# The lead of an attention-and-MLP kernel: a copy and two read-outs change engine, three loads change places, and an order is planned anew

## The chip, the cores and the metric

The kernel runs on one core of a Trainium2 chip. The core has a matrix engine (PE), a vector engine (DVE), an activation engine (ACT) and a general one (POOL); SP issues the DMAs. Each engine works through its own list of instructions in order, and waits on semaphores for the others. The metric is the device time of one execution in microseconds (us); less is better.

## The reference, cut to what matters

Two batches of 8 heads, 768 positions, 64 values per head. Each query attends to a window of 31 neighbours and, besides, to 24 block summaries (the maximum of the keys, the mean of the values, over blocks of 32). The result goes through two MLPs.

```python
k_sum = k.reshape(B, H, nb, 32, D).max(axis=3)
v_sum = v.reshape(B, H, nb, 32, D).mean(axis=3)
scores_l = scale * q @ k.T                    # masked to |i - j| < 16
scores_s = scale * q @ k_sum.T + log(32)
a = softmax(concat(scores_l, scores_s))
x = a @ concat(v, v_sum)                      # 1536 tokens x 512
x = (relu(x @ w_in) ** 2) @ w_out             # MLP 1
out = silu(x @ w_in2) @ w_out2                # MLP 2
```

## The kernel before, in words

The 12 attention tiles of a batch hold 64 queries each; their keys are 96 neighbours and the 24 summaries, 120 in all. The first eight tiles are the **lead**: nothing else can run before them, since MLP 1 works on their 512 tokens (`gemm1 0` is its first product, tile `h`). The other tiles are done in pairs between the products of MLP 1. After the lead PE has work without a gap.

One tile of the lead passes through these steps. The names are those of the planner; in brackets the names that the profile shows.

- `psl (g, hp)` on PE: scores of tile g for a pair of heads (`pss<-kws,qrlead`), two matmuls. `kwl (hp, i)` on ACT lays the window keys of tiles 0 to 3 or 4 to 7 side by side (`kws<-t_ksum`); `ksum` and `ksl` on DVE put the summaries of the keys beside them.
- `ttl (g, hp)` on DVE: mask and minimum, read from PSUM (`T<-pss,cst_sb`; the mask is in `cst_sb`). `exl (g, hp)` on ACT: exponential and its sum (`T<-T,m`). `ze`, `rc`, `nt` on DVE: guard, reciprocal and four scalings (`z`, `r`, `T<-T,r`).
- `psa g` on PE: four transposes (`psa<-cst_sb,T`). `a g`: the copy of them out of PSUM (`a<-psa`, 120x512), on ACT.
- `vs c`, c from 0 to 5, on PE: the sums of the values (`psv<-vrows,share`), for all tiles together. `vmean 0` and `vmean 1` on ACT copy them four times each into rows 96 to 119 of `vlead`, for tiles 0 to 3 and 4 to 7 (`vlead<-psv`, 24x2048); in the code that is a source whose outer step is zero.
- `av g` on PE: eight products (`av<-a,vlead`). `xh g` on ACT and `xl g` on DVE: the high and the low part of the result (`xt<-av`). `gemm1 0` reads all eight pairs.

Beside this, weights are prepared in steps `sc` (ACT), `sh` and `st2` (DVE), `hi` (ACT, `wi` or `wo`) and `lo` (DVE); `vfm` on ACT (`vfr<-vlead`, 24x512) puts the sums of the values in place for later tiles; `vend` on PE, and `vfc` on DVE behind it (`vfr<-vsum`), do the like for the second batch, whose first tiles begin with `av 12`.

The order of all this is set by `first_order`. It lists every step with its engine, a duration, a due time and what it needs, and then plays the program through: whenever an engine is free it takes, among the steps that could start soonest, the one with the earliest due time. The instructions are then written out in that order. A due time or a duration that changes thus moves other steps too. Loads are all issued by SP, in the order of a list. Before the first scores PE runs ten matmuls of zeros (`idle_out`), and between the groups of scores six and four more.

Of the kernel before, what the change touches and what calls it, by code (L numbers as in the profile page):

```python
# [10 lines left out]
F32 = mybir.dt.float32  # L11
F32R = mybir.dt.float32r
AF = mybir.ActivationFunctionType
# [9 lines left out]
P = 128  # L23
# [22 lines left out]
NLEAD = 8  # L46
# [7 lines left out]
NRING = 8  # L54
NMIXED = 2
FIRST2 = 1
DEC1 = 14
# [9 lines left out]
def first_order():  # L67
# [6 lines left out]
    def op(eng, name, arg, dur, due, deps=(), bank=None, kb=0):  # L74
        o = index[name, arg] = dict(eng=eng, name=name, arg=arg, dur=dur, due=due + shift.get(name, 0), deps=list(deps), bank=bank, kb=kb,
                                    n=len(ops))
        ops.append(o)
# [7 lines left out]
    def pair(name, g):  # L85
        return g if g < NLEAD + 2 * (name == "pss") else g // 2 * 2
# [12 lines left out]

    for i, (name, arg, kb) in enumerate([("kt", 0, 393), ("q", 0, 524), ("kt", 1, 393), ("cst", 0, 250), ("kt", 2, 393),  # L100
                                         ("kt", 3, 393), ("q", 1, 524), ("vr", 0, 524), ("vr", 1, 524), ("vr", 2, 524),
                                         ("vl", 0, 1150), ("vl", 1, 1150)]):
        load(name, arg, kb, -100 + i)
    for hp in range(NHP):
        op("vec", "ksum", hp, 1.0, -50 + hp, [("kt", hp, 0)])
        for i in range(NLEAD // NGRP):
            op("act", "kwl", (hp, i), .5, -50 + hp + 51 * i, [("kt", hp, 0)])
            op("vec", "ksl", (hp, i), .13, -50 + hp + 48 * i, [("ksum", hp, 0)])
    for c in range(6):
        op("pe", "vs", c, .92, 2.7 + .1 * c, [("vr", c // 2, 0)])  # L110
    for i in range(NLEAD // NGRP):
        op("act", "vmean", i, 1.9, -5, [("vs", c, M) for c in range(6)] + [("vl", i, 0)] * 0)
    for i in range(NVF):
# [9 lines left out]
    for g in range(NFIRST):  # L123
# [24 lines left out]
        visit("psa", g, .62, due - 2, [("nt", g, -.1)], ("att", "a", g))  # L148
        op("act", "a", g, .56, due, [("psa", pair("psa", g), M)] + [("av", pair("av", g - 2), M)] * (g >= NLEAD + 2))
        values = [("vl", g // NGRP, 0), ("vmean", g // NGRP, A)] if g < NLEAD else [("vf", g, 0), ("vfm", g % NVF, A)]  # L150
# [6 lines left out]
    for i, (x, s) in enumerate(chunks):  # L157
# [4 lines left out]
        if i >= NSPL:  # L162
            y = chunks[i - NSPL]
            before += [("lo", y, A)] + [("scr", y[1], 0)] * (y[0] == "wo")
        op("act", "sc", (x, s), .59, due, [("raw", (x, s), 0)] + before)
        op("vec", "sh", (x, s), .35, due, [("raw", (x, s), 0)])
        op("vec", "st2", (x, s), .61, due, [("sh", (x, s), 0), ("sc", (x, s), A)])
# [14 lines left out]

    free = dict(sp=0.0, act=0.0, vec=0.0, pool=2.0, pe=5.6)
    end, banks, moved = {}, dict(att=[], acc=[]), 2.0
# [37 lines left out]
def kernel(  # L222
# [239 lines left out]
    def a_copy(g):  # L462
        d = st[g]
        a = d.pop("pa")[0:NK].rearrange("p c q -> p (c q)")
        if g >= NLEAD:
            d["a"] = p2.tile([P, 512], F32, tag="a", bufs=2, name=f"a{g}")
        copy(act, d["a"][0:NK], a)

# [133 lines left out]
    def first_block():  # L602
# [6 lines left out]
        psv = ps_h.tile([P, DM], F32, tag="h", name="psv0")  # L609
        vec.memset(idle_in.bitcast(F32), 0.0)  # L610
        def turn(n):
            for _ in range(n):
                mm(idle_out, idle_in[:, 0:P], idle_in, start=True, stop=True)
# [64 lines left out]
        def vmean(i):  # L678
            means = psv[NWIN:NK]
            copy(act, vlead[NWIN:NK, i * NGRP:i * NGRP + NGRP].rearrange("p g h d -> p g (h d)"),  # L680
                 bass.AP(means.tensor, means.offset, [means.ap[0], [0, NGRP], means.ap[1]]))
# [474 lines left out]
```

## Time and profile before

| | |
|---|---|
| time, median of 3 runs | 587.97 us (587.80 to 588.05) |
| the profiled execution, its own time | 587.53 us |
| its span, first to last instruction | 585.7 us |
| PE busy | 577.5 us, 99% |
| DVE, ACT, POOL busy | 384.8, 363.1, 95.3 us |
| the chain that ended last, by engine | PE 95%, ACT 2%, DVE 1%, DMA 1% |
| granted TensorE clock, mean | 1.000 |

How to read it: the span is 1.8 us shorter than the time of the same execution; what lies around it is start and end. The chain is followed back from the last instruction, at each step to what released it. The share of an engine over the whole span says little on the lead, which is the first 6% of it; the stretches of 10 us and the rows in order of time, shown below, do.

### The profile page before, as it was taken

Reading aid. Unit: us, or ns where it says so; the run is one execution under the profiler, and the core shown is the slowest. Engines: PE = TensorE matmul, PEld = TensorE weight load, DVE = VectorE, ACT = ScalarE, POOL = GpSimd, SP = SyncE. Lnnn points to the kernel's source line nnn. Section 1 sums busy time; section 2 is a strip of 40 time slices with the busy share of each in tenths; the row PEclk is TensorE's granted clock in tenths of the full one; section 3 lists DMA queues with packets and bytes.
Section 4 is the critical chain, followed back from the end, with each engine's and each line's share of the span. In section 5 each row is a group of like instructions: output and inputs, shape, how many; then the busy total and the mean of one; then the engine's idle time right before and its main releaser. Section 6 shows DMA issues by size and latency. Waiting matters only on the chain.

```text
span 585.7 us, 9518 instructions
## 1 busy us (share of the span) xinstructions
PE 577.5 (99%) x3300; PEld 489.4 (84%) x3300; DVE 384.8 (66%) x975; ACT 363.1 (62%) x848; POOL 95.3 (16%) x99
## 2 busy tenths in 40 slices
PE   8989999999999999999999999999999999999997
PEld 7578888878888888888888889999889888889995
DVE  6989899852867556286553688676665765666641
ACT  6999797954736554385455677665555655555541
POOL 0001101103553443076342300000000000000000
PEclk9999999999999999999999999999999999999999
DMA  9999989753988879526870112242248311111002
GB/s 316 303 305 307 346 289 325 250 166 127 319 304 293 288 258 340 178 92 196 287 261 28 36 55 73 90 145 90 91 144 358 145 36 37 36 37 35 23 17 107
DMA packets 42240, 104.42 MB, mean 178 GB/s; under 512 B 4560, under 2 KB 11856, under 8 KB 42192
## 3 DMA queue, kind: packets, MB, share of 16 engines
q1 hardware_dynamic: 42192, 103.81, 52.2%
q8 instruction: 26, 0.43, 0.3%
q14 instruction: 22, 0.18, 0.1%
HBM read 78.37 MB, written 25.43 MB: 177 GB/s over the span
## 4 chain that ended last, share of the span: by engine, by line
PE 95%; ACT 2%; DVE 1%; DMA 1%; issue 0%; DVEq 0%; ACTq 0%
PE acc L256 45%; PE h L256 23%; PE hx L256 11%; PE hz L256 6%; PE pss L256 4%; PE hy L256 3%; PE psa L460 2%; PE av L256 1%; ACT T L423 1%; ACT vlead L260 1%; DMA t_ksum<-in_kT_dram 1%; DVE xt L264 0%; PE idle_out L256 0%; PE psv L256 0%; ACT L260 0%; ACT a L260 0%
## 5 line engine op out<-in xcount | busy, mean ns | idle before, releaser
L256 PE MATMUL h<-xt,wi 128*128 128x512 f32 x576 | 143.0, 394 | 1.2 <-ACT xt L260 0.9
L256 PE MATMUL acc<-g,wo 128*128 128x512 f32 x576 | 140.4, 391 | 0.0
L256 PE MATMUL acc<-wq,g 128*128 128x512 f32 x576 | 134.3, 390 | 0.0
L256 PEld LDWEIGHTS h<-xt,wi 128*128 128x128 f32 x576 | 106.7, 188 | 24.7 <-ACT xt L260 1.0
L256 PEld LDWEIGHTS acc<-g,wo 128*128 128x128 f32 x576 | 107.4, 188 | 22.5 <-issue 0.2
L256 PEld LDWEIGHTS acc<-wq,g 128*128 128x128 f32 x576 | 107.8, 188 | 21.9 <-DVE wq L264 0.3
L264 DVE TENSOR_TENSOR g<-r,g 128x512 fp32r<-128x512 f32 x48 | 38.5, 802 | 68.4 <-ACT g L260 37.5
L264 DVE TENSOR_TENSOR r_s<-v,r_s 128x256 fp32r<-128x256 f32 x48 | 20.6, 432 | 66.6 <-ACT r_s L260 66.6
L260 ACT ACTIVATE e<-hx 128x384 f32<-128x384 f32 x32 | 15.7, 492 | 61.9 <-PE hx L256 61.8
L423 ACT ACTIVATE T<-T,m 128x120 f32<-128x120 f32 x96 | 36.6, 383 | 8.4 <-DVE m L418 8.3
L260 ACT ACTIVATE g<-s 128x384 fp32r<-128x384 f32 x64 | 32.9, 517 | 10.3 <-DVE s L264 10.2
L256 PE MATMUL hx<-x_t,r_s 128*128 128x384 f32 x192 | 38.5, 335 | 0.0
L264 DVE TENSOR_TENSOR g<-s,g 128x384 fp32r<-128x384 f32 x64 | 35.1, 553 | 2.6 <-ACT g L260 1.1
L256 PEld LDWEIGHTS hx<-x_t,r_s 128*128 128x128 f32 x192 | 33.8, 188 | 0.3
L968 ACT ACTIVATE s<-e 128x384 f32<-128x384 f32 x48 | 25.0, 522 | 8.7 <-DVE e L264 6.4
L264 POOL TENSOR_TENSOR wo<-c_wo,wo 128x512 fp32r<-128x512 f32 x16 | 25.9, 1621 | 26.2 <-ACT wo L260 25.8
L261 POOL COPY qd<-qr 128x256 f32<-128x256 f32 x14 | 12.5, 910 | 104.7 <-DMA qr<-in_qW_dram 47.9
L555 ACT ACTIVATE r<-h 128x512 f32<-128x512 f32 x16 | 9.5, 596 | 30.9 <-PE h L256 30.9
L264 DVE TENSOR_TENSOR s<-e,s 128x384 f32<-128x384 f32 x48 | 26.4, 550 | 0.3 <-ACT s L968 0.3
L264 POOL TENSOR_TENSOR r<-r 128x512 f32<-128x512 f32 x16 | 16.8, 1052 | 51.5 <-ACT g L560 51.5
L454 DVE TENSOR_SCALAR T<-T,r 128x120 f32<-128x120 f32 x96 | 24.4, 318 | 0.5
L260 ACT ACTIVATE wo<-c_wo 128x512 fp32r<-128x512 f32 x32 | 20.1, 627 | 4.9 <-DVE c_wo L311 4.9
(112 smaller groups left out, 900.5 us busy)
## 6 DMA issues: line engine op xcount, KB each, us to landing
raw_wi<-in_w_in_dram SPq DMA_DIRECT2D x16, 512.0 KB, 5.8
raw_wo<-in_w_out_dram SPq DMA_DIRECT2D x16, 512.0 KB, 5.8
raw_wp<-in_w_out_dram SPq DMA_DIRECT2D x16, 512.0 KB, 4.8
split<-wo SPq DMA_DIRECT2D x16, 512.0 KB, 3.3
raw_wj<-in_w_in_dram SPq DMA_DIRECT2D x16, 512.0 KB, 4.7
wo<-split SPq DMA_DIRECT2D x16, 512.0 KB, 3.5
c<-scr_dram SPq DMA_DIRECT2D x32, 256.0 KB, 2.7
scr_dram<-c_wo SPq DMA_DIRECT2D x16, 256.0 KB, 4.0
```

Source lines behind the costliest of these rows:

```text
L256: pe.matmul(o, l, r, **kw)
L260: return act.activation(out=o, in_=i, func=AF.Copy, scale=scale)
L261: return eng.tensor_copy(out=o, in_=i)
L264: return eng.tensor_tensor(out=o, in0=a, in1=b, op=op)
L423: act.activation(out=d["T"][:, c], in_=d["T"][:, c], func=AF.Exp, bias=d["m"][:, c:c + 1], scale=-1.0, accum_out=d["z"][:, c:c + 1])
L454: vec.tensor_scalar(out=T[:, c], in0=T[:, c], scalar1=r[:, c:c + 1], scalar2=None, op0=ALU.mult)
L460: pe.transpose(ps[0:NK, c], d["T"][:, c], id_sb)
L555: act.activation(out=r, in_=h, func=AF.Relu)
L968: act.activation(out=s, in_=src, func=AF.Sigmoid)
```

## The change

1. In the list of loads `cst` (the mask and constants) moves from the fourth place to the second.
2. An exponential of one column, `early`, is written at the start of the program, so that ACT's table load stands ahead of the wait for the first keys and not behind it.
3. `vmean 1` goes from ACT to DVE and takes its source from `vlead` of tile 0 (SBUF), where `vmean 0` put it, not from PSUM.
4. `a 6` and `a 7` go from ACT to DVE.
5. Numbers of the planner: `kwl` of the second half of the tiles has the due time of the first half; `vs` is due earlier and by smaller steps; `sc` and `sh` of the weights after the first wait for `nt 7`; PE counts as free from 4.8 on, not 5.6.

```diff
+AVEC = (6, 7)
...
-    for i, (name, arg, kb) in enumerate([("kt", 0, 393), ("q", 0, 524), ("kt", 1, 393), ("cst", 0, 250), ("kt", 2, 393),
+    for i, (name, arg, kb) in enumerate([("kt", 0, 393), ("cst", 0, 250), ("q", 0, 524), ("kt", 1, 393), ("kt", 2, 393),
...
-            op("act", "kwl", (hp, i), .5, -50 + hp + 51 * i, [("kt", hp, 0)])
+            op("act", "kwl", (hp, i), .5, -50 + hp, [("kt", hp, 0)])
...
-        op("pe", "vs", c, .92, 2.7 + .1 * c, [("vr", c // 2, 0)])
+        op("pe", "vs", c, .92, 1.5 + .05 * c, [("vr", c // 2, 0)])
...
-        op("act", "vmean", i, 1.9, -5, [("vs", c, M) for c in range(6)] + [("vl", i, 0)] * 0)
+        op("vec" if i else "act", "vmean", i, 1.25 if i else 1.82, -5, [("vmean", 0, A)] if i else [("vs", c, M) for c in range(6)])
...
-        op("act", "a", g, .56, due, [("psa", pair("psa", g), M)] + [("av", pair("av", g - 2), M)] * (g >= NLEAD + 2))
+        op("vec" if g in AVEC else "act", "a", g, .65 if g in AVEC else .56, due, [("psa", pair("psa", g), M)] + [("av", pair("av", g - 2), M)] * (g >= NLEAD + 2))
...
-        op("act", "sc", (x, s), .59, due, [("raw", (x, s), 0)] + before)
-        op("vec", "sh", (x, s), .35, due, [("raw", (x, s), 0)])
+        op("act", "sc", (x, s), .59, due, [("raw", (x, s), 0)] + before + [("nt", NLEAD - 1, 0)] * (i > 0))
+        op("vec", "sh", (x, s), .35, due, [("raw", (x, s), 0)] + [("nt", NLEAD - 1, 0)] * (i > 0))
...
-    free = dict(sp=0.0, act=0.0, vec=0.0, pool=2.0, pe=5.6)
+    free = dict(sp=0.0, act=0.0, vec=0.0, pool=2.0, pe=4.8)
...
-        copy(act, d["a"][0:NK], a)
+        copy(vec if g in AVEC else act, d["a"][0:NK], a)
...
+        early = first_p.tile([P, 1], F32, tag="early", name="early")
+        act.activation(out=early, in_=idle_in[:, 0:1].bitcast(F32), func=AF.Exp)
...
-            means = psv[NWIN:NK]
-            copy(act, vlead[NWIN:NK, i * NGRP:i * NGRP + NGRP].rearrange("p g h d -> p g (h d)"),
+            means = vlead[NWIN:NK, 0].rearrange("p h d -> p (h d)") if i else psv[NWIN:NK]
+            copy(vec if i else act, vlead[NWIN:NK, i * NGRP:i * NGRP + NGRP].rearrange("p g h d -> p g (h d)"),
```

What this does to the order is seen best on two engines, near the end of the lead. On PE, from `psa 4` on, before (`psv` is `vs`, `psa_485` and `psa_497` are `psa 6` and `psa 7`):

```order
L460 MATMUL psa_439<-cst_sb,T_160 120x128 x4
L256 MATMUL psv_124<-vrows_197,share 24x512
L460 MATMUL psa_457<-cst_sb,T_165 120x128 x4
L256 MATMUL psv_124<-vrows_197,share 24x512
L256 MATMUL psv_124<-vrows_199,share 24x512 x2
L460 MATMUL psa_485<-cst_sb,T_170 120x128 x4
L460 MATMUL psa_497<-cst_sb,T_175 120x128 x4
L256 MATMUL av_504<-a_141,vlead 64x64 x8
```

The same place now (`pss_469` is the scores of tile 7, `psa_472` is `psa 6`):

```order
L461 MATMUL psa_430<-cst_sb,T_162 120x128 x4
L257 MATMUL psv_124<-vrows_199,share 24x512
L257 MATMUL psv_124<-vrows_201,share 24x512
L461 MATMUL psa_451<-cst_sb,T_167 120x128 x4
L257 MATMUL psv_124<-vrows_201,share 24x512
L257 MATMUL pss_469<-kws_0_140,qrlead_111 64x120 x2
L461 MATMUL psa_472<-cst_sb,T_172 120x128 x4
L257 MATMUL pss_469<-kws_0_140,qrlead_111 64x120 x2
L257 MATMUL pss_469<-kws_1_141,qrlead_111 64x120 x4
L257 MATMUL av_491<-a_143,vlead 64x64 x8
```

One `vs` now stands ahead of `psa 0` and the others end sooner, the scores of tile 7 come behind the last `vs`, and `psa 7` (not in these rows) has gone behind `av 4`. On DVE, the rows ahead of the first `xl` (`xt`) before:

```order
L264 TENSOR_TENSOR wi_469<-c_wi_455,wi_469 128x512
L443 TENSOR_SCALAR z_173<-z_173 128x4
L446 RECIPROCAL r_174<-z_173 128x4
L454 TENSOR_SCALAR T_170<-T_170,r_174 128x120 x4
L443 TENSOR_SCALAR z_178<-z_178 128x4
L446 RECIPROCAL r_179<-z_178 128x4
L454 TENSOR_SCALAR T_175<-T_175,r_179 128x120 x4
L308 TENSOR_SCALAR raw_wo_211<-raw_wo_211 128x512
L308 TENSOR_SCALAR raw_wi_213<-raw_wi_213 128x512
L264 TENSOR_TENSOR xt_88<-av_504,xt_88 128x4x64
```

The same now, as far as the first `xl`; with the waits of the built program, the first `ttl` of tile 7 (the first row of `T_177`) waits for PE, `a 6` waits for nothing of its own, the next `ttl` waits for PE again, and the last two for nothing:

```order
L265 TENSOR_TENSOR wi_458<-c_wi_447,wi_458 128x512
L419 ISA T_177,m_179<-pss_469,cst_sb 128x120
L419 ISA m_179 128x1
L262 COPY a_173<-psa_472 120x512
L419 ISA T_177,m_179<-pss_469,cst_sb 128x120
L419 ISA m_179 128x1
L419 ISA T_177,m_179<-pss_469,cst_sb 128x120
L419 ISA m_179 128x1
L419 ISA T_177,m_179<-pss_469,cst_sb 128x120
L419 ISA m_179 128x1
L262 COPY vlead<-vlead 24x2048
L265 TENSOR_TENSOR xt_88<-av_491,xt_88 128x4x64
```

The four `ttl` of tile 7, `a 6` and `vmean 1` now stand between `lo` of the first weights and `xl 0`. The rest of DVE's lead is:

```order
L265 TENSOR_TENSOR xt_88<-av_503,xt_88 128x4x64
L455 TENSOR_SCALAR T_177<-T_177,r_181 128x120 x4
L265 TENSOR_TENSOR xt_88<-av_513,xt_88 128x4x64
L265 TENSOR_TENSOR xt_88<-av_526,xt_88 128x4x64
L309 TENSOR_SCALAR raw_wo_213<-raw_wo_213 128x512
L265 TENSOR_TENSOR xt_88<-av_543,xt_88 128x4x64
L262 COPY a_178<-psa_554 120x512
L312 SCALAR_TENSOR_TENSOR c_wo_572<-c_wo_572,raw_wo_213 128x512
L265 TENSOR_TENSOR xt_88<-av_562,xt_88 128x4x64
L265 TENSOR_TENSOR xt_88<-av_575,xt_88 128x4x64
L309 TENSOR_SCALAR raw_wi_215<-raw_wi_215 128x512
L265 TENSOR_TENSOR xt_88<-av_589,xt_88 128x4x64
```

It holds `nt 7`, two `sh`, `a 7` and `st2` between the `xl`, where before it held two `sh`, a small copy and `st2`.

## Rows read from the trace of the kernel before

**Rows 1.** Windows: stretch, its us, busy us (count) of PE, PEld, DVE, ACT, POOL, granted clock, DMA share, GB/s.

```profile
20.00:30.00 10.00, 9.27 (x47) 3.57 (x46) 8.27 (x45) 9.73 (x33) 0.00 (x0) 1.00 1.04 334
30.00:40.00 10.00, 8.22 (x142) 6.98 (x139) 8.20 (x20) 9.89 (x21) 0.00 (x0) 1.00 0.85 261
40.00:60.00 20.00, 20.00 (x110) 16.13 (x109) 19.04 (x59) 18.51 (x43) 1.82 (x1) 1.00 0.96 333
```

**Rows 2.** Chain that ended last, in order of time: start us, us, what.

```profile
23.15 0.60 ACT a L260
...
25.82 1.89 ACT T L423 x10
...
27.73 3.63 ACT vlead L260 x2
```

**Rows 3.** PE in order of time: start us, us, work, count, in brackets idle time before.

```profile
5.79 1.22 PE L256 MATMUL pss<-kws,qrlead 64*64 64x120 f32 x16
...
8.53 1.59 PE L256 MATMUL pss<-kws,qrlead 64*64 64x120 f32 x16
...
11.19 4.03 PE L256 MATMUL pss<-kws,qrlead 64*64 64x120 f32 x60
15.15 0.65 PE L460 MATMUL psa<-cst_sb,T 128*120 128x128 f32 x4
15.97 0.74 PE L256 MATMUL pss<-kws,qrlead 64*64 64x120 f32 x8 [0.17 <-ACT T L423]
```

**Rows 4.** PE in order of time, end of the lead.

```profile
27.30 0.81 PE L460 MATMUL psa<-cst_sb,T 128*120 128x128 f32 x4
...
35.29 0.50 PE L256 MATMUL h<-xt,wi 128*128 128x512 f32 x1 [0.90 <-ACT xt L260]
36.12 1.20 PE L256 MATMUL h<-xt,wi 128*128 128x512 f32 x4 [0.33 <-DVE xt L264]
```

**Rows 5.** ACT in order of time.

```profile
3.92 1.28 ACT L260 ACT_TABLE_LOAD   x1 [3.92 <-DMA t_ksum<-in_kT_dram]
5.21 0.94 ACT L260 ACTIVATE kws<-t_ksum 128x384 f32<-128x384 f32 x2
```

**Rows 6.** DVE in order of time.

```profile
19.32 0.28 DVE L418 CUSTOM_DVE_ANT_0 T<-pss,cst_sb 128x120 f32<-128x120 f32 x1
...
19.52 0.28 DVE L418 CUSTOM_DVE_ANT_0 T<-pss,cst_sb 128x120 f32<-128x120 f32 x1
...
28.15 0.86 DVE L454 TENSOR_SCALAR T<-T,r 128x120 f32<-128x120 f32 x4
28.93 0.43 DVE L308 TENSOR_SCALAR raw_wo<-raw_wo 128x512 int32<-128x512 int32 x1
...
31.80 1.09 DVE L264 TENSOR_TENSOR xt<-av,xt 128x256 fp32r<-128x256 f32 x3 [2.11 <-ACT xt L260]
32.81 0.42 DVE L308 TENSOR_SCALAR raw_wo<-raw_wo 128x512 int32<-128x512 int32 x1
33.14 0.41 DVE L264 TENSOR_TENSOR xt<-av,xt 128x256 fp32r<-128x256 f32 x1
...
34.71 0.69 DVE L311 SCALAR_TENSOR_TENSOR c_wo<-c_wo,raw_wo 128x512 int32<-128x512 int32 x1
35.32 0.75 DVE L264 TENSOR_TENSOR xt<-av,xt 128x256 fp32r<-128x256 f32 x2
```

**Rows 7.** DVE copies by tile: count, ns least/median/most; the last by lines, mean ns.

```profile
L261 DVE COPY vfr<-vsum x2: 414/417/420, 117.2 to 117.5; 24x512 f32<-24x512 f32 x2
L261 DVE COPY xr<-acc x6: 679/688/692, 144.1 to 340.1; 128x512 f32<-128x512 f32 x6
L261 DVE COPY kw<-ksum 128x96 f32<-128x96 f32 x1 | 0.2, 201 | 0.0
```

**Rows 8.** DMA: issue of the first queries on SP, then KB and us to landing.

```profile
1.18 0.42 SPq L633 DMA_DIRECT2D qrlead<-in_qW_dram  x1
qrlead<-in_qW_dram SPq DMA_DIRECT2D x1, 512.0 KB, 4.1
```

## The prediction, made before the changed kernel ran

> **What bounds the kernel now.** I read the windows first. From 40 us on PE is busy in every microsecond (20.00 of 20), at a granted clock of 1.00, the upper of its two levels, and so it goes on; in the two stretches before, PE has gaps and ACT has none worth the name: 9.73 and 9.89 of 10 us [rows 1]. So the time is set by the moment from which `gemm1 0` runs without a stop, plus a stream of matmuls that the change does not shorten. A row of PE gives that moment: 36.12 us, after a first matmul at 35.29 and 0.33 us of waiting for the last `xl` [rows 4]. Whatever the change does in the lead counts as a shift of 36.12 and as nothing else, unless it makes a new hole later.
>
> Then the chain in order of time, to see what released what. Up to about 23 us its pieces are mostly PE's; PE's own rows show why: from 11.19 on it works without a pause but one of 0.17 us [rows 3], until `psa 6` ends at 27.30 + 0.81 = 28.11 [rows 4]. From 23.15 the chain is ACT's: `a` copies, ten pieces of exponentials, and from 27.73 the two `vmean`, 3.63 us [rows 2]. Behind these come the `xh` and `xl`, and DVE, which had been idle 2.11 us for the first `xh`, ends its last `xl` at 35.32 + 0.75 = 36.07 [rows 6]. The reader is to keep two facts: PE is full from 11 to 28 us, and DVE has a hole of 2.1 us before 31.80 just where ACT is full.
>
> **The change, part by part.** The early edits first. ACT's table load takes 1.28 us from 3.92 on, behind the first keys, and the first `kwl` starts at 5.21 [rows 5]. With the load ahead, it starts at 3.92. But the first scores also need the queries, which landed at 1.18 + 4.1 = 5.28 [rows 8]. They are now third in the queue, behind `cst`. The keys that released ACT had landed about 3.9 [rows 5], so the 512 KB of queries took some 1.4 us; by that rate, worked out from these rows, `cst` with its 244 KB costs 0.67 us. The first scores then start near 6.0 and not 5.79 [rows 3]: 0.2 later, not 1.3 earlier. That 0.2 is given back: the second group of 16 took 1.59 where the first took 1.22 [rows 3], 0.37 us of waiting for DVE, which with the mask at hand is further on. PE's matmuls of zeros stay in its list, so its full stretch begins at about 11.1 to 11.2 as before. Taken at nothing, bounds -0.4 and +0.3.
>
> The Trainium skill, page "ScalarE: Activation LUTs", section "What ACT_TABLE_LOAD costs", puts a switch of tables at 2.66 us, 1.28 for the load and 1.38 for draining the engine. The trace shows the first part alone: the next instruction starts 0.01 us after the load. By the page the edit would take 2.66 us off ACT's start, by the row 1.28; either way the queries are later, and the sum stays.
>
> The middle. PE's list from 11.2 us to the second `psl` of tile 7 holds what it held before up to `psa 6`, but for the last two `psl` of tile 7. Sixty records of that kind took 4.03 us, and a matmul here makes two records, so one is 0.134 us and the four matmuls left out are 0.54. From 28.11 that gives 27.57. Without any of the waits that before still has in it (0.17 [rows 3], and `psa 6` at 0.81 [rows 4] where `psa 0` took 0.65 [rows 3], 0.16), 27.2; with some new ones, since the `vs` now pushes between the scores and the four banks of scores come free by DVE, 27.9. I take 27.8, near the upper end: PE has no slack with which to make up a bank that comes late. In the built order the first `ttl` of tile 7 waits for PE and `a 6` behind it has no wait of its own, so that one wait covers `psa 6` and the `psl` that follows; DVE is done with what stands ahead by about 28.15 - 0.4 - 0.8 = 26.95 (before, `nt 7` began at 28.15 [rows 6], behind `ze` and `rc` of its tile, 0.4, and the four `ttl`, 0.8, that now come later), and stands idle until 27.8.
>
> The end, on DVE, by distances between starts, which is what an engine's list costs. `ttl`: 0.20. `nt`: 0.78. `xl`: 1.01 for three, 0.335 each. `sh`: 0.33. `st2`: 0.61 [rows 6]. New are two kinds. `vmean 1` copies 2048 values per partition in SBUF. A copy of 512 took 0.417 and one of 96, whose source also has an outer step of zero, 0.201 [rows 7]: 0.52 ns a value, so 0.417 + 1536 x 0.00052 = 1.22 us. The other bound is DVE's fp32 work with one value a cycle: 256 values 0.41 and 512 values 0.69 [rows 6], 1.09 ns a value, which makes 0.69 + 1.68 = 2.37. I take 1.22, since the row of 96 has the same kind of source. Start to start it is 0.08 less, as in the rows above: 1.14. `a 6` and `a 7` read PSUM as `xr<-acc` does, 0.688 for the same 512 values [rows 7], 0.61 start to start; the lower bound is 0.417.
>
> The sum. From 27.8: the first `ttl`, then the last two `psl`, which write the bank that it reads (0.20 + 0.54 + about 0.25 for the two hand-overs, estimated from the distances of starts between engines; `a 6`, 0.61, lies beside them): 1.0. Three `ttl` 0.6. `vmean 1` 1.14. Eight `xl` 2.68. `ze` and `rc` of tile 7 with the wait between them, 0.3. `nt 7` 0.78. Two `sh` 0.66. `a 7` 0.61. `st2` 0.61. The tail of the last `xl` beyond its share 0.08. That is 8.46, and the last `xl` ends at 36.26. Before, it was 36.07. So +0.19; ahead of it nothing is hidden by other work, as DVE never waits in this stretch.
>
> What does the gain of 1.8 + 2 x 0.6 us on ACT [rows 2] do, then? It is real, and ACT's `xh 7` comes earlier than before even with two `vfm` and a third `sc` now ahead of it; but it hands the last place to DVE, whose list takes on 1.14 + 1.22 of copies and the four `ttl` and `nt` of tile 7 that before were over by 28.93 [rows 6]. The last `xh` I put at 35.4 to 36.0: `vmean 0` from 26.5 (two `psl`, 0.5, and `psa 6`, 0.65, now lie between the last `vs` and 27.8), then 1.8, four exponentials 1.5, eight `xh` 2.6, two `vfm` 1.1, three `sc` 1.7, plus waits for DVE's `ttl`, about 0.6. That is just short of DVE.
>
> Later steps. `vend` now stands behind `gemm1 12`, 2.7 us later; the copies that need it were over at 117.5 + 0.42 = 117.9 [rows 7] in a list that was full around them, so not all of the 2.7 falls on `av 12`. I count 0, with up to 0.5 as the upper bound.
>
> The profiled execution took 587.53, its span 585.7; +0.2 makes 587.7. The median stands 0.44 above that execution, so I put the shift on the median: 587.97 + 0.2 = 588.2.
>
> **The rivals.** A, the forecast: DVE's list ends the lead, 588.2.
>
> B, faster: PE gets through without waits and the first `ttl` of tile 7 is not held. Then it starts at 27.2 or before, and the last two `psl` and `a 6` overlap with it, worth 0.6 and 0.5 us: the last `xl` ends near 35.2, -0.9, 587.1. If the early stretch also begins 0.4 us sooner, 586.7. For it speaks that ACT loses 3.0 us of work [rows 2] and that DVE's hole before 31.80 is 2.11 [rows 6]; against it, that PE is full from 11.19 to 28.11 and no matmul is taken from it.
>
> C, slower: `vmean 1` runs at one value a cycle and takes 2.37, not 1.22, and stands in DVE's list with nothing beside it: +1.15 more, 589.3. It decides the sign by 0.2% once the copy takes over about 2.2 us. Against it speaks the row of 96 values [rows 7]; for it, that no row shows so wide a copy of a repeated source. The Trainium skill, page "VectorE: DVE Perf Modes", section "Mode 2×_2P — use both read ports for one tensor", has such a copy split in two halves along its outermost dimension, one per read port, and that dimension is here the repeated one. By that rule the copy takes 1.2 and C falls; no run here shows it at this width.
>
> D: the lead gains what B gains in part, and `vend` or a weight that is ready later gives it back as a hole in PE at some 42 or 119 us; 587.6 to 588.7.
>
> **How the numbers follow.** About 0.2%, 1.18 us, is what a measurement of this kernel can tell from no change. A 0.60, all within. B 0.22: half of it beyond 1.18. C 0.10, nearly all beyond. D 0.08, within but for 0.02. That makes faster 0.12, within 0.2% 0.76, slower 0.12. The range reaches from B's 587.0 to C's 589.3; outside lie part of B and of C, under 2 in 10.
>
> **What would show it.** In the profile of the changed kernel: the first scores near 6.0 and PE full from 11.2; the first `ttl` of tile 7 at 27.6 to 27.9 after an idle time of DVE that PE ended; `vlead<-vlead` 24x2048 on DVE at 1.2 us; both `a<-psa` on DVE at 0.69; DVE without a gap from there to its last `xl` at 36.1 to 36.5, and PE's `gemm1 0` waiting for it; no wait of PE after that. I am wrong if that first `ttl` stands before 27, if ACT's `xh 7` is what `gemm1 0` waits for, or if PE shows a hole later.

## The result: 0.5% slower, and outside the range

| | before | after |
|---|---|---|
| median of 21 runs each | 588.05 us (587.24 to 589.91) | 590.86 us (588.74 to 594.37) |
| after over before | | 1.0052 [1.0040, 1.0064] |
| the profiled execution, its own time | 587.53 us | 590.86 us |
| its span | 585.7 us | 589.1 us |

The forecast was 588.2 us with a range of 587.0 to 589.3. The kernel came out at 590.86, slower by over 0.2%, which had a chance of 0.12; and by a mechanism that none of the rivals named. The profiled execution of the kernel after has its median time. That of the kernel before took 587.53, 0.5 us less than its median, so the rows differ by more than the medians do: 3.4 us of span against 2.8. The rows below find 2.6 of the 3.4 before PE's full stretch begins, and 0.8 at the end of the lead. Of the experiments further down, one execution each of b11 and e5 took some 2034 us and is left out of the ratios; in b11 it was the profiled one, so b12 is the same kernel again.

PE of the kernel after, in order of time (start us, us, work, count, in brackets the idle time before and what ended it):

```profile
1.46 4.63 PE L257 MATMUL idle_out<-idle_in 128*128 128x512 f32 x10 [1.46 <-DVE idle_in L611]
7.36 1.88 PE L257 MATMUL pss<-kws,qrlead 64*64 64x120 f32 x16 [1.27 <-DMA qrlead<-in_qW_dram]
9.16 2.41 PE L257 MATMUL idle_out<-idle_in 128*128 128x512 f32 x6
11.51 1.22 PE L257 MATMUL pss<-kws,qrlead 64*64 64x120 f32 x16
12.66 1.20 PE L257 MATMUL idle_out<-idle_in 128*128 128x512 f32 x4
13.78 2.20 PE L257 MATMUL pss<-kws,qrlead 64*64 64x120 f32 x32
...
39.09 5.97 PE L257 MATMUL h<-xt,wi 128*128 128x512 f32 x24 [0.90 <-ACT xt L261]
44.98 1.22 PE L257 MATMUL pss<-kw,qr 64*64 64x120 f32 x16
```

Two rows of the kernel before that these are measured against, and that [rows 3] leaves out:

```profile
1.46 4.22 PE L256 MATMUL idle_out<-idle_in 128*128 128x512 f32 x10 [1.46 <-DVE idle_in L610]
...
6.93 1.66 PE L256 MATMUL idle_out<-idle_in 128*128 128x512 f32 x6
```

**The early part.** Before, the first scores started at 5.79 without a wait and the full stretch at 11.19 [rows 3]. Now the first scores wait 1.27 us for the queries and start at 7.36, +1.57. The same 16 then take 1.88 us instead of 1.22, and six matmuls of zeros take 9.16 to 11.51, 0.39 each, where after 12.66 four take 12.66 to 13.78, 0.28 each. Only the wait of 0.37 in the second group is gone, as predicted (1.22 now, 1.59 before). So the full stretch starts at 13.78: 1.57 + 0.66 + 0.75 - 0.37 = 2.61 by these four, 2.59 by the two starts. Some of this is the luck of the profiled execution of the kernel before: its last two zeros were already fast, and so were all its scores. In b2, b9, b12 and b13, whose first loads and first matmuls are in the same order, the ten zeros took 4.63 or 4.64 us, and the full stretch began at 11.64 to 11.80. Against those the early part costs 2.0 to 2.1 us.

**The end of the lead.** From the start of the full stretch to `gemm1 0` it was 36.12 - 11.19 = 24.93 us. The next scores behind the 24 `h` now start at 44.98. In the kernel before, that is this row of PE:

```profile
41.56 1.22 PE L256 MATMUL pss<-kw,qr 64*64 64x120 f32 x16
```

So the product runs +3.42 us later, of which 3.42 - 2.59 = 0.83 are the end of the lead.

**Behind the lead nothing changes.** A window of the kernel after, from 40 us on (stretch, its us, busy us of PE, PEld, DVE, ACT, POOL, granted clock, DMA share, GB/s):

```profile
40.00:60.00 20.00, 20.00 (x110) 16.12 (x109) 19.72 (x58) 16.26 (x35) 0.65 (x1) 1.00 0.95 317
```

PE is as full as before [rows 1], and in the windows from 60 to 580 us it is busy in 519.97 of 520 us; the 3.42 us are simply carried to the end.

The chain that ended last names both places. Of the kernel after, first 46 us, in order of time (start us, us, what):

```profile
1.65 5.57 DMA qrlead<-in_qW_dram
...
34.02 0.63 ACT vfr L261
...
35.35 0.63 ACT vfr L261
...
36.41 0.69 ACT c_wo L304
37.10 0.56 ACT c_wi L304
...
38.21 0.55 ACT c_wo L304
38.76 0.28 ACT xt L261
```

At its start stands the load of the queries, 5.57 us from its issue; at its end ACT, between whose last `xh` stand two `vfm` and three `sc` of the weights. In the kernel before, ACT's two `vmean` stood there [rows 2].

### The profile page after: what moved, and what is told of

Same layout as the page of the kernel before. It is cut to its first block, busy times and chain, and to the rows that moved or that the text cites. A ratio compares the mean times of both kernels' runs of the same rounds, so it can differ in the third digit from the quotient of the medians.

```text
span 589.1 us, 9515 instructions
## 1 busy us (share of the span) xinstructions
PE 579.6 (98%) x3300; PEld 490.7 (83%) x3300; DVE 388.2 (66%) x978; ACT 361.8 (61%) x846; POOL 94.2 (16%) x99
## 4 chain that ended last, share of the span: by engine, by line
PE 96%; ACT 2%; DMA 1%; DVE 0%; issue 0%; SPq 0%; DVEq 0%
PE acc L257 45%; PE h L257 23%; PE hx L257 11%; PE hz L257 6%; PE pss L257 4%; PE hy L257 3%; PE psa L461 2%; PE av L257 1%; ACT T L424 1%; DMA qrlead<-in_qW_dram 1%; PE psv L257 1%; PE idle_out L257 1%; ACT xt L261 0%; ACT vfr L261 0%; ACT c_wo L304 0%; DVE T L419 0%
## 5 line engine op out<-in xcount | busy, mean ns | idle before, releaser
L419 DVE CUSTOM_DVE_ANT_0 T<-pss,cst_sb 128x120 f32<-128x120 f32 x96 | 21.7, 275 | 7.5 <-PE pss L257 7.2
```

Source lines behind the costliest of these rows:

```text
L419: vec.tensor_tensor_reduce(out=d["T"][:, c], in0=d["ps"][:, c], in1=cst_sb[:, kind * NK:kind * NK + NK], scale=-0.125, scalar=3.0e38, op0= ...
```

## The experiments

Each ratio is to runs of the kernel before on the same chip.

| label | what it is | median us | over before |
|---|---|---|---|
| b1_cst_second | before, mask second | 590.70 | 1.0046 [1.0034, 1.0058] |
| b8_q_third | before, second keys second | 591.27 | 1.0050 [1.0038, 1.0062] |
| b14_cst_warm | b1 and 16 matmuls of zeros | 589.57 | 1.0026 [1.0017, 1.0036] |
| e3_warm | after, 14 matmuls of zeros | 590.15 | 1.0032 [1.0021, 1.0044] |
| e1_loads_old | after, loads as before | 590.35 | 1.0042 [1.0030, 1.0054] |
| e2_q_cst | after, queries second, mask third | 589.25 | 1.0022 [1.0011, 1.0033] |
| b2_early | before, table load first | 587.93 | 0.9997 [0.9989, 1.0006] |
| e4_all_but_loads_vs | after, old loads, old `vs` | 588.73 | 1.0014 [1.0005, 1.0024] |
| b9_vs | before, new due time of `vs` | 593.51 | 1.0094 [1.0080, 1.0108] |
| b10_vs_moves | b9 and the copies on DVE | 591.95 | 1.0063 [1.0052, 1.0075] |
| b11_vmean_only | before, `vmean 1` on DVE | 587.39 | 0.9986 [0.9977, 0.9995] |
| b12_vmean_only | the same once more | 587.56 | 0.9990 [0.9982, 0.9999] |
| b13_vmean_sh_later | b12, three steps of DVE later | 587.65 | 0.9994 [0.9985, 1.0002] |
| e5_hold_back | before, copies on DVE, weights held back | 588.25 | 1.0005 [0.9996, 1.0015] |

The theory: the queries in third place cost the early part, and the new order of the lead's end costs the rest. The rivals: the early part is the new order of PE or DVE and not the load; the end is the copy on DVE itself.

### The place of the mask alone: b1_cst_second

The order of all engines is that of before; only the first four loads change places in the written-out list.

```diff
-    return [(o["name"], o["arg"]) for o in ops]
+    names = [(o["name"], o["arg"]) for o in ops]
+    first = [('kt', 0), ('cst', 0), ('q', 0), ('kt', 1)]
+    for i, x in zip(sorted(names.index(x) for x in first), first):
+        names[i] = x
+    return names
```

> The kernel before with the mask loaded second, ahead of the queries; nothing else of the change. 'Queries': the same pause of PE ahead of the first scores and the same slow matmuls after it, +2.4 to +2.9 us, 590.4 to 591.0, and runs spread over some us. 'List': no more than 0.3 us from the kernel before, since its end of the lead is untouched.

Measured: +2.6 us, nearly the loss of the whole change. PE of b1 in order of time:

```profile
7.73 1.88 PE L260 MATMUL pss<-kws,qrlead 64*64 64x120 f32 x16 [1.64 <-DMA qrlead<-in_qW_dram]
9.54 2.25 PE L260 MATMUL idle_out<-idle_in 128*128 128x512 f32 x6
...
14.39 2.83 PE L260 MATMUL pss<-kws,qrlead 64*64 64x120 f32 x40
...
39.32 3.94 PE L260 MATMUL h<-xt,wi 128*128 128x512 f32 x16 [0.34 <-DVE xt L268]
```

The first rows are those of the changed kernel: a wait for the queries, slow scores, slow zeros. The end of the lead is untouched: 39.32 - 14.39 = 24.93, as before. The load's place alone makes the early loss: the full stretch starts at 14.39.

### Is it the mask, or the third place? b8_q_third

As b1, with `first = [('kt', 0), ('kt', 1), ('q', 0), ('cst', 0)]`: the second keys, not the mask, go ahead of the queries.

> The kernel before with the second keys ahead of the first queries (keys, keys, queries, mask), nothing else. It asks whether the queries are late because they are third, or because the mask is ahead of them. If loads simply follow each other at their pace in the kernel before (384 KB in 1.0 us, 512 KB in 1.4): queries at 6.3, first scores 0.5 later than before, the pause of PE 0.6 us; if PE's matmuls keep their pace +0.2 to +0.5 us, with the clock lost +1.5 to +2. If a load of 512 KB in third place is slow as it was behind the mask (2.7 us): queries at 7.6 or later, +2.5 us or more.

Measured: 591.27, no better than b1. The queries' piece of the chain of b8:

```profile
1.65 5.90 DMA qrlead<-in_qW_dram
```

and of b1:

```profile
1.65 5.94 DMA qrlead<-in_qW_dram
```

In third place the queries land 5.6 (after) to 6.7 us (b14) after their issue. In second place it was 4.1 before [rows 8], 4.0 in e4, 4.1 in b2, 4.7 in e1 and 4.9 in e2, from an issue 0.47 us sooner. So the step from second to third place costs far more than the 0.67 us by which I had priced the move from the size of the mask. That sizes have no part in it isn't shown: the 140 KB that b8 has more ahead than b1 would be 0.4 us by that rate, and the four runs with the same mask ahead (after, b1, e3, b14) differ among themselves by 1.1 us.

### What of it is wait, and what is clock? b14_cst_warm and e3_warm

```diff
-WARM = 10
+WARM = 16
```

in b1's kernel, and 14 in the kernel after: more matmuls of zeros while the queries are on their way.

> The kernel before with the mask second, as b1_cst_second, and 16 matmuls of zeros ahead of the first scores and not 10. 'Queries' with its clock: the queries as late as in b1, 7.2 to 8.2, but the scores and the matmuls of zeros behind them at full pace (1.2 and 1.7 us), so that only the wait is left: +1.2 to +1.9 over the kernel before, 589.2 to 589.9, with runs closer together than b1's. If the clock has no part: 590.5 to 591.3, as b1.

> The changed kernel with 14 matmuls of zeros ahead of the first scores and not 10, so that PE is busy until the queries land at about 7.2. It parts the late queries from the clock. 'Queries' with its clock: first scores still at 7.3 to 7.8, but the 16 records of scores in 1.2 us and not 1.9 and the six matmuls of zeros in 1.7 and not 2.4: 1.2 to 1.4 us earlier than the changed kernel, 589.0 to 589.6, and the runs close together again. If the clock has no part in it: no gain, 590.5 to 591.5. 'List': no gain either.

Measured: b14 wins back 1.1 us of b1's 2.6 (589.57 against 590.70), as expected. e3 wins 0.7 us of the change's 2.8 and missed its 589.0 to 589.6; its interval overlaps that of the change a little. PE of b14:

```profile
1.46 6.70 PE L260 MATMUL idle_out<-idle_in 128*128 128x512 f32 x16 [1.46 <-DVE idle_in L614]
8.45 1.22 PE L260 MATMUL pss<-kws,qrlead 64*64 64x120 f32 x16 [0.30 <-DMA qrlead<-in_qW_dram]
9.60 1.66 PE L260 MATMUL idle_out<-idle_in 128*128 128x512 f32 x6
```

and of e3:

```profile
1.46 4.83 PE L257 MATMUL idle_out<-idle_in 128*128 128x512 f32 x14 [1.46 <-DVE idle_in L611]
8.37 1.22 PE L257 MATMUL pss<-kws,qrlead 64*64 64x120 f32 x16 [2.08 <-DMA qrlead<-in_qW_dram]
9.52 1.67 PE L257 MATMUL idle_out<-idle_in 128*128 128x512 f32 x6
...
13.41 2.20 PE L257 MATMUL pss<-kws,qrlead 64*64 64x120 f32 x32
```

The scores and the six zeros behind them are back at 1.22 and 1.67 us (after: 1.88 and 2.41), although the queries came later still: 6.7 and 6.6 us after their issue. From the first scores to the full stretch e3 takes 13.41 - 8.37 = 5.04 us, the kernel after 13.78 - 7.36 = 6.42: 1.4 us of slow matmuls. That the added zeros did this is shown by b14, not by e3: in e3's profiled execution 14 zeros took hardly longer than ten take in the kernel after (4.83 against 4.63), so the level had risen before the tenth, and ten would probably have done there. In b14 nearly all of the 16 are slow, 6.70 us for them, and ten would have been over near 6.1, two microseconds before its queries landed. What is left, 1.5 us in b14 by the medians, and 2.06 less the 0.83 of the lead's end in e3, is the wait itself, which no zeros remove. Fewer than ten zeros were not tried.

### The old loads under the new order: e1_loads_old and e2_q_cst

The loads of the kernel after are put in the old order (e1), or with the queries second and the mask third (e2), in the manner of b1; all engines keep their new order.

> The changed kernel with the first four loads in the order of before (keys, queries, keys, mask), all instructions of the engines as in the changed kernel. Theory 'queries' (the first scores wait for queries that land late behind the mask, PE stands still 1.3 us, and its matmuls then run at the lower clock level until 10.8 us): first scores at 5.8 us, no pause ahead of them, the six matmuls of zeros behind them in 1.7 us and not 2.4; everything 2.6 us earlier than in the changed kernel, first ttl of tile 7 near 28.0, gemm1 0 without a stop from 36.3 to 36.6, time 588.0 to 588.5, and the runs as close together as those of before. Rival 'list' (DVE's new list at the end of the lead is the cost, the start would be made up later): 590 to 591 as the changed kernel.

> The changed kernel with the queries second and the mask third (keys, queries, mask, keys), nothing else moved. 'Queries': first scores at 5.8 us as with the old order, the mask landed at about 6.0, so the first ttl at 6.5 to 7 and not 8.1; DVE and ACT are ahead by 1 us early on, but PE's list is full from 11.2, so the end of the lead gains 0.3 us at most over the old order: 587.7 to 588.4. 'List': 590 to 591.

Both missed. For e1 I expected 588.0 to 588.5, and it stayed at 590.35; for e2 587.7 to 588.4, and it took 589.25. The first scores are early again, but PE of e1 goes on like this:

```profile
5.98 1.22 PE L261 MATMUL pss<-kws,qrlead 64*64 64x120 f32 x16 [0.19 <-DMA qrlead<-in_qW_dram]
7.13 1.67 PE L261 MATMUL idle_out<-idle_in 128*128 128x512 f32 x6
10.52 1.22 PE L261 MATMUL pss<-kws,qrlead 64*64 64x120 f32 x16 [1.72 <-DVE kws L266]
11.68 1.71 PE L261 MATMUL idle_out<-idle_in 128*128 128x512 f32 x4
13.32 2.99 PE L261 MATMUL pss<-kws,qrlead 64*64 64x120 f32 x32
```

In the new order of DVE three `ttl` stand ahead of the second `ksum`, and the `ttl` need the mask. With the mask in fourth place DVE sits until it lands, as DVE of e1 shows:

```profile
8.57 0.28 DVE L423 CUSTOM_DVE_ANT_0 T<-pss,cst_sb 128x120 f32<-128x120 f32 x1 [3.50 <-DMA cst_sb<-in_cst_dram]
```

The loss has moved from the queries to the mask, with a pause of PE and slow zeros (1.71 for four) behind it again. A window of e1 prints the lower level there (stretch, its us, PE busy, granted clock, DMA share, GB/s):

```profile
12.00:15.50 3.50, 3.50 (x26) 0.52 1.06 341
```

e2 has both early, wins 1.6 us of 2.8 and leaves +1.2: its full stretch starts at 11.85 (+0.66; 0.41 us of waiting for the queries and 0.54 for `kws` are among it), its 24 `h` at 37.13 and the scores behind them at 43.02, which is +0.80 at the end of the lead, like the 0.83 of the change. So the early part is the load order and the order of DVE that was planned with it, and the end of the lead is a loss by itself.

### The table load alone: b2_early

The two lines of `early` in the kernel before.

> The kernel before with the early exponential alone (the table load ahead of the first keys). 'Queries' (the first scores wait for their queries, so an earlier table load has nothing to hand on): first kwl at 3.9, first scores still at 5.7 to 5.8, time within 0.3 us of the kernel before; the queries land 4.1 us after their issue as before. Rival 'early' (the load moved to the front disturbs the first transfers, since in two runs with it and the queries in second place they landed after 4.7 and 4.9): queries later than 5.6 us and +0.5 us or more.

Measured: no difference, 0.9997 [0.9989, 1.0006]. PE of b2 says why:

```profile
1.46 4.64 PE L256 MATMUL idle_out<-idle_in 128*128 128x512 f32 x10 [1.46 <-DVE idle_in L610]
6.02 1.43 PE L256 MATMUL pss<-kws,qrlead 64*64 64x120 f32 x16
```

`kwl` starts 1.3 us sooner (3.94, 5.21 before [rows 5]), but PE is on its ten matmuls of zeros until about 6 and goes to the scores without a wait.

### The end of the lead: e4, b9, b10

e4 is the change without the loads and without the new numbers of `vs` and `pe`:

```diff
-("kt", 0, 393), ("cst", 0, 250), ("q", 0, 524), ("kt", 1, 393),
+("kt", 0, 393), ("q", 0, 524), ("kt", 1, 393), ("cst", 0, 250),
...
-        op("pe", "vs", c, .92, 1.5 + .05 * c, [("vr", c // 2, 0)])
+        op("pe", "vs", c, .92, 2.7 + .1 * c, [("vr", c // 2, 0)])
...
-    free = dict(sp=0.0, act=0.0, vec=0.0, pool=2.0, pe=4.8)
+    free = dict(sp=0.0, act=0.0, vec=0.0, pool=2.0, pe=5.6)
```

b9 is the kernel before with the new numbers of `vs` alone, and b10 is b9 with `vmean 1`, `a 6` and `a 7` on DVE as in the change.

> The whole change but the order of the loads and the due times of vs (and PE free from 5.6): early table load, vmean 1 and a 6, a 7 on DVE, kwl due early, sc and sh after nt 7. The scores of tile 7 then stand ahead of the vs as before. 'Order' (the new place of the vs is what the end of the lead pays for, the moves of work cost nothing): 587.8 to 588.4, gemm1 0 without a stop from 35.9 to 36.4. Rival 'moves' (DVE's copies are the cost): 588.8 to 589.3.

> The kernel before with the new due times of vs alone. The scores of tile 7 come behind the last vs, psa 7 behind av, and ACT still has both vmean: 'Order' expects the end of the lead 2.5 to 4 us later (PE waits some 2.5 us for nt 7 near 35), 590.5 to 592. If the place of the vs is of no account: 587.9 to 588.5.

> The kernel before with vmean 1, a 6 and a 7 on DVE and with the new due times of vs, loads and table load as before. 'Order': the scores of tile 7 come behind the last vs, PE waits for DVE near 28 and 31, gemm1 0 without a stop 0.8 to 1.3 us later than before: 588.8 to 589.3. If the vs due times cost nothing: 587.8 to 588.3.

e4 is 0.14% slower; its 588.73 lies between the two ranges that I had given. Its full stretch starts at 11.51, its second `h` at 37.08: 25.57 us against 24.93, +0.64. ACT of e4 near the end:

```profile
29.94 0.70 ACT L304 ACTIVATE c_wo<-raw_wo 128x512 f32<-128x512 f32 x1
30.67 0.63 ACT L261 ACTIVATE vfr<-vlead 24x512 f32<-24x512 f32 x1
```

The 1.8 us that the second `vmean` leaves free are filled by the planner with `sc` and `vfm`; between `vmean 0` and the last `xh` there now stand three `sc`, a `hi` and two `vfm`, where the kernel before had one `sc` and two `a` behind its second `vmean`, and PE's first `h` waits 1.17 us for ACT.

b9 is the worst of all, +5.5 us: a due time of `vs` alone. The four scores of tile 7 go behind the last `vs`, `ttl`, `nt`, `psa 7` and `a 7` follow late, and PE of b9 stands idle three times, for 2.42, 1.08 and 0.48 us. The first:

```profile
35.86 0.90 PE L460 MATMUL psa<-cst_sb,T 128*120 128x128 f32 x4 [2.42 <-DVE T L454]
```

With the copies on DVE (b10) 1.6 us of it come back. In both the level falls behind the pauses (b10: 0.57 in this window); b9's:

```profile
39.00:43.00 4.00, 3.41 (x7) 0.50 0.94 324
```

Both came out slower than I had expected (590.5 to 592 for b9, 588.8 to 589.3 for b10), and neither expectation had a fall of the level in it. So the earlier `vs` harms by itself, and the copies on DVE give a part of that back. In the change as a whole the earlier `vs` weighs little: from the full stretch to the scores behind the first product e4, without it, loses 42.52 - 11.51 - 30.37 = 0.64 us, and the change, with it, 0.83 (30.37 is 41.56 - 11.19, before). Which of its other steps keeps the change from the 45.57 - 12.28 - 30.37 = 2.92 us that b10 loses in the same stretch was not tried.

### The copy alone: b11 and b12_vmean_only, b13, e5

The order is that of before; only the engine and the source of `vmean 1` change.

```diff
-            means = psv[NWIN:NK]
-            copy(act, vlead[...
+            means = vlead[NWIN:NK, 0].rearrange("p h d -> p (h d)") if i else psv[NWIN:NK]
+            copy(vec if i else act, vlead[...
```

> The kernel before with vmean 1 alone on DVE, copied from vlead of tile 0, every step in its old place in the list (the planner is not told). It asks whether the copy is worth moving where DVE has its hole. 'Order' (the moved copy pays if nothing is planned anew around it): xh 0 at 30.2 and not 31.4, the copy on DVE at 29.6 to 30.9, the last xl 0.4 to 0.9 earlier than before, 587.2 to 587.7; part of it may come back as PE waiting for the second weights near 39. Rival 'moves' (DVE's copy costs what ACT's copy cost): 587.9 to 588.5.

> The same kernel as b11_vmean_only, for its rows: vmean 1 alone on DVE, every step in its old place. 'Order': 587.2 to 587.7 again; the copy at 29.6 to 30.9 for 1.22 us, xh 0 at about 30.2, the last xl ending at 35.2 to 35.7 (36.07 before), with DVE busy from the copy to the last xl. 'Moves': 587.9 to 588.5.

Measured: 0.9986 [0.9977, 0.9995] and 0.9990 [0.9982, 0.9999]: faster by about 0.1%, the best of all kernels here, though by less than the 0.2% that the prediction takes as the measure. (The profiled execution of b12, 587.66, is no shorter than that of before, as its full stretch began 0.61 us later; the rows are compared from there on.) PE of b12:

```profile
11.80 4.03 PE L256 MATMUL pss<-kws,qrlead 64*64 64x120 f32 x60
...
30.27 4.16 PE L256 MATMUL av<-a,vlead 120*64 120x64 f32 x128 [0.26 <-ACT vlead L260]
...
36.13 5.51 PE L256 MATMUL h<-xt,wi 128*128 128x512 f32 x23 [0.34 <-DVE xt L264]
```

All eight `av` now run without a gap, and from the full stretch to the second `h` it is 36.13 - 11.80 = 24.33 us, 0.60 less than before. Why not the 1.8 that ACT was spared? ACT of b12 now waits for PE:

```profile
31.00 1.32 ACT L260 ACTIVATE xt<-av 128x256 fp32r<-128x256 f32 x3 [0.78 <-PE av L256]
```

and of before, where the products lay ready:

```profile
31.39 0.94 ACT L260 ACTIVATE xt<-av 128x256 fp32r<-128x256 f32 x3
```

The two `vmean` took 3.63 [rows 2], the one that is left takes 1.87: 1.76 less the wait of 0.78 and the slower pace of the first three `xh`, 0.38, is 0.60. What ACT does behind them is as before.

b13 puts two `sh` and a small copy of DVE behind the last `xl`:

```diff
+    for x, y in [(('sh', ('wo', 1)), ('xl', 7)), (('sh', ('wi', 2)), ('xl', 7)), (('kwc', 8), ('xl', 7))]:
+        names.remove(x)
+        names.insert(names.index(y) + 1, x)
```

> As b12, with two sh and one small copy of DVE (0.33, 0.33 and 0.12) moved behind the last xl. If DVE's list around the copy sets the end of the lead, the last xl ends another 0.3 to 0.6 earlier; the second weights then become the limit and PE waits 0.2 to 0.4 us near 39 for them, so the time is 587.0 to 587.6, little better than b12. If ACT sets it: no earlier, 587.4.

It brings nothing more: `xl` starts no sooner, and DVE now shows waits of 0.19 and 0.34 us for ACT's `xt`. DVE's list was not the limit of b12; ACT's was. e5 takes the copies on DVE, the early table load, and lets `vfm`, `sc` and `sh` of the later weights wait for the last `xh` or `xl`:

```diff
-        op("act", "vfm", i, .6, tile_due(NLEAD) - 10 + i, [("vmean", 0, 0)])
+        op("act", "vfm", i, .6, tile_due(NLEAD) - 10 + i, [("vmean", 0, 0), ("xh", NLEAD - 1, 0)])
```

> The kernel before with the early table load, vmean 1 and a 6, a 7 on DVE, loads and vs as before, and with vfm, sc and sh of the weights after the first held back until the last xh (sh: the last xl). It asks whether the time that ACT is relieved of goes to steps that are not due. If so, the lead ends earlier: gemm1 0 without a stop from 35.0 to 35.6 (36.1 before, 37.1 with the same moves and nothing held back), but the second weights are then late and PE waits 0.8 to 1.3 us near 38 to 41, and perhaps once more near 120: 587.6 to 589.0. If the moves are slow by themselves: gemm1 0 not before 36.5.

Measured: 588.25, no difference. PE of e5:

```profile
35.41 3.25 PE L257 MATMUL h<-xt,wi 128*128 128x512 f32 x12 [0.48 <-ACT xt L261]
38.81 0.73 PE L257 MATMUL h<-xt,wi 128*128 128x512 f32 x2 [0.15 <-ACT wi L261]
40.28 2.57 PE L257 MATMUL h<-xt,wi 128*128 128x512 f32 x10 [0.74 <-DVE wi L265]
```

`gemm1 0` starts 35.41 - 11.92 = 23.49 us after the full stretch, 0.6 sooner than the 35.29 - 11.19 = 24.10 of before; but the second product then waits 0.15 and 0.74 us for its weights, which were held back. What ACT and DVE do for the weights in the lead is needed 3 us later, so holding it back moved the wait and did not remove it. `a 6` and `a 7` on DVE were not tried without the rest.

## Why the prediction was wrong, point by point

**What bounds the kernel: right.** From `gemm1 0` on PE is full, and the whole difference is a shift of that moment.

**The queries: the step that failed.** The prediction put "cst costs 0.67", the first scores "near 6.0", and the early part "at nothing, bounds -0.4 and +0.3". The queries landed at 1.65 + 5.57 = 7.22, not at 5.95, and the early part cost 2.59 us by the rows of the two profiled executions, 2.0 to 2.1 against b2, b9, b12 and b13. Two things were wrong in it. First, the price: 1.4 us for 512 KB was read from a load in second place and taken for a rate. b1 and b8 show that the third place costs much more than that, with 244 KB between the first keys and the queries as with 384 KB. A row of DVE in the kernel before could have warned, as it shows the third load of that kernel:

```profile
6.87 0.95 DVE L649 TENSOR_REDUCE ksum<-t_ksum 128x24 f32<-128x768 f32 x1 [1.68 <-DMA t_ksum<-in_kT_dram]
```

There 384 KB landed about 1.5 us behind the 512 KB of the queries (5.28 [rows 8]): 3.9 ns a KB, not 2.7. By that row 244 KB would have cost 0.95 and 512 KB 2.0 us behind 3.9: a landing at 6.9, near the 7.22 measured, and an upper bound of +1 at least. Second, the consequence: I let a late load cost its own delay. But PE, whose ten zeros had taken 4.63 us, 0.46 each, then paused, had not reached its upper level, and worked at the lower one until 10.8 us (how the trace shows it stands in the last section); b14 and e3 put that part at 0.7 to 1.4 us. No term and no bound of the sum had the clock in it.

**The stall given back: right.** The 0.37 us before the second scores are gone.

**The table load: right.** Nothing in the sum, nothing in b2. The trace again shows the load alone, 1.28 us, and the next ACT instruction 0.01 us behind it; the longer price of the Trainium skill, page "ScalarE: Activation LUTs", section "What ACT_TABLE_LOAD costs", shows in no run here.

**PE's list in the middle: right.** From the full stretch to the first `ttl` of tile 7 I had 27.8 - 11.15 = 16.65 us; it is 30.61 - 13.78 = 16.83. PE ended DVE's idle time before it, as predicted. DVE of the kernel after from there:

```profile
30.61 0.28 DVE L419 CUSTOM_DVE_ANT_0 T<-pss,cst_sb 128x120 f32<-128x120 f32 x1 [1.01 <-PE pss L257]
...
30.82 0.69 DVE L262 COPY a<-psa 120x512 f32<-120x512 f32 x1
31.74 0.28 DVE L419 CUSTOM_DVE_ANT_0 T<-pss,cst_sb 128x120 f32<-128x120 f32 x1 [0.24 <-PE pss L257]
...
32.47 1.22 DVE L262 COPY vlead<-vlead 24x2048 f32<-24x2048 f32 x1
33.73 0.42 DVE L265 TENSOR_TENSOR xt<-av,xt 128x256 fp32r<-128x256 f32 x1
...
39.07 0.42 DVE L265 TENSOR_TENSOR xt<-av,xt 128x256 fp32r<-128x256 f32 x1
```

**The new copies: right.** `vmean 1` took 1.22 us, the value taken, and `a` 0.69. Rival C, one value a cycle, falls. The rule of the Trainium skill, page "VectorE: DVE Perf Modes", section "Mode 2×_2P — use both read ports for one tensor", agrees in its result.

**DVE's list: short by 0.42.** It was to take 8.46 us to the end of the last `xl` and takes 39.49 - 30.61 = 8.88. The two hand-overs to PE took 1.13 instead of 1.0, the three `ttl` 0.73 instead of 0.6, the copy 1.26 from start to start instead of 1.14: it starts when the `ttl` ahead has ended (32.47) and the next one starts when it has ended (33.73), where I had let copies overlap by 0.08 as other instructions do. The rest, 5.76, is as summed (5.72). With 0.18 from PE's list and the forecast's own +0.19 that makes 0.79 of the 0.83 measured.

**Who ends the lead: wrong by its own sign, and nearly a tie.** I wrote that I would be wrong if ACT's last `xh` is what `gemm1 0` waits for, and the first `h` does wait for it (0.90 us). ACT's last `xh` ends at 39.04, DVE's last `xl` at 39.49, and DVE was busy with a `sh` until 39.06: both lists are level there, and the 0.45 us between them lie in the forecast's span for it (0.3 to 0.9). But ACT's last `xh` did not come "earlier than before": counted from the full stretch it ends 39.04 - 13.78 = 25.26 us later, where before it was 35.23 - 11.19 = 24.04. (The forecast's own 35.4 to 36.0 for it was already later than that 35.23.) What I had mis-judged is how little of ACT's gain would last: in the new order the planner fills it with `sc` and `vfm` (e4), and in the old one `xh` waits for `av` (b12).

**No later hole: right**, the `vend` term included.

**The sum.** +0.2 was forecast and +3.42 found. 2.59 of the gap are the early part, with the failed step; 0.6 are the small terms of the end. By the medians the loss is 2.81; the execution from which I had read 36.12 ran 0.5 us below its median. Had the early part been right, I estimate 588.2 + 0.6 = 588.8; e4, which has the old loads and the old `vs`, took 588.73.

One thing is open. The 21 runs of the changed kernel spread over 5.6 us, those of before over 2.7, and the records of the slowest of them show a mean granted clock of 0.990 to 0.996, those of the fastest 1.000. The profiled execution has no fall of the level between 13.78 and the end of its matmul stream. That in the others the level falls at the end of the lead, as in b9 and b10, is argued and not shown. The moment of the first rise may spread the runs too (10.8 us in the kernel after, 13.9 in b8); the mean granted clock does not have it in it, and that is not shown either.

## What to carry to other kernels

Price a load that is moved one place back in the queue by the row of the load that stood in that place: here that row led to a landing at 6.9 and the rate of an earlier load to 5.95, and 7.22 was measured. When what waits for it is a matrix engine whose clock has not risen yet, the price has a second part, the slow matmuls behind the pause. Loads and the engines' order belong together: the same list of loads under an order planned for another one (e1) loses nearly as much as the wrong list, 2.3 us against 2.8. A copy that is moved off the engine that ends a stage brings what the next engine or the next weights leave over, here 0.6 us of 1.8, and a planner that fills the freed time with work due later can turn that into a loss.

## What the runs showed of the hardware

**The level of TensorE's clock and a pause at the start.** The trace lists the granted clock only from the moment at which it first stands at the upper level; ahead of that it has no entry, and the column prints 1.00 although the matmuls are slow. In the kernel after the list begins at 10.8 us. Up to there the matmuls of zeros start 0.427 us apart (to 5.46, and from 9.76 to 10.61), and from 10.95 on 0.23. The same 0.427 stands in e1 between the zeros at 12.33 and 12.76, where the column prints 0.52, the lower level. So in the first microseconds the durations have to be read, not the column.

The list begins between 4.4 (e3) and 7.4 us (b14) in the twelve profiled executions in which PE was at work from 1.46 on until then, and at 10.8, 10.9 and 13.9 in the three in which PE, still at the lower level, first waited 1.27 to 1.64 us for the queries (after, b1, b8). The first 16 scores took 1.22 to 1.59 us in the twelve, and the six zeros behind them 1.63 to 1.67; in the three it was 1.88, and 2.25 to 2.93. A wait of 2.08 us behind the rise (e3) left the scores at 1.22.

**The third load.** In second place the 512 KB of queries landed 4.0 to 4.9 us after their issue (ten profiled executions), in third place 5.6 to 6.7 (five), with 384 KB or with 244 KB between; the mask, 244 KB, took 5.1 us from its issue when it was third (e2) and 3.3 when it was second (after); and the load ahead of them had landed at 1.18 + 3.3 = 4.5 us in the kernel after, so they ended 2.7 us behind it, where in second place they ended 1.4 us behind the keys. Why the third waits so long is open. The DMA engines were not idle: from 4 to 6 us their mean busy share was 0.86 to 1.11 in the five, but they moved 225 to 257 GB/s, where in the ten it was 251 to 370.

**A copy on DVE from a repeated source**, fp32 in SBUF, 24 partitions x 2048 values: 1.22 to 1.23 us, 0.6 ns a value, in every run that has it.
